# First pairs of a retention and feed-forward kernel: q loaded and transposed like k, zero products in fp32, first weight casts in halves

## The chip, the core and the metric

The kernel runs on one core of one Trainium2 chip. The metric is the device time of one execution in microseconds (us), as the median of several runs of the same program. The engines are TensorE (PE, its weight loads shown as PEld), VectorE (DVE), ScalarE (ACT), GpSimd (POOL) and SyncE (SP), which here only issues transfers. Matrix products write to PSUM, the accumulator memory; everything else lies in SBUF or in device memory.

## What is computed

A decayed linear attention (one decay per head), and then a bilinear feed-forward over its tokens:

```python
gamma = 1.0 - 2.0 ** (-5.0 - np.arange(H))          # q, k, v: [4, 8, 768, 64]
for t in range(S):
    state = gamma[None, :, None, None] * state + np.einsum('bhd,bhe->bhde', k[:, :, t], v[:, :, t])
    y[:, :, t] = scale * np.einsum('bhd,bhde->bhe', q[:, :, t], state)
x = y.transpose(0, 2, 1, 3).reshape(B * S, H * D)   # [3072, 512]
out = (x @ w_a) * (x @ w_b) @ w_out                 # w_a, w_b: [512, 1536]; w_out: [1536, 512]
```

All inputs and the output are fp32; the products on TensorE take bf16 operands.

## The kernel before

**Tiling.** The 3072 tokens are 24 slots of 128 tokens, six for each batch entry. The decay is put into the operands: k is multiplied by gamma to the power of -(t - 384) and q by gamma to the power of (t - 384) over 8, from tables (`ktab`, `qtab`), so that within a batch entry attention is a masked product of q and k (`scores`), its product with v (`intra`), and the product of q with a running state (`inter`, `update`). The feed-forward goes over token tiles of `TILES = [4, 2, 4, 4, 4, 4, 2]` slots: for each of 12 blocks of the inner dimension `ffn_a` and `ffn_g` make the two products (four TensorE instructions each, ACT copies the one, DVE multiplies it with the other), and `ffn_out` makes the output rows of a slot from the 12 blocks.

**The first batch entry** is treated in three pairs of slots (`load_pair`, `casts2`, `flip2`, `scores2`, `update2`, `inter2`, `intra2`, `leave2`), 256 tokens each. k and v are loaded with two neighbouring tokens to a partition (`(p two)`, pieces of 512 bytes), so that a half of a pair is the even or the odd tokens (`par`). q is loaded otherwise: partition (b, h) holds 16 consecutive tokens of one head (NJ = 16; two transfers of 256 KB each with pieces of 2 KB, lines 96 to 102). Its scaling (line 240) takes its factors from a table with one row to such a partition, which `lane_table` (lines 158 to 179) makes from the identity matrix, and it is transposed by plain products with a selecting matrix `pick` (line 394): 32 weight loads and 32 products to a pair, against 8 and 8 for k (line 387). The columns of q's transposed tile, and so those of the scores, of the attention's result and the rows of the output tile, stand in (j, b) order; `masks` and the output's address pattern follow that.

**Output rows.** The six slots of the first two token tiles are stored in that permuted order through SP's queue. `ffn_out` puts such a store in `held` (line 529), and `store` issues it at the next step. The others go through ACT's queue.

**What sets the order.** Each engine works strictly in the order in which the program is written: `seq` ties every instruction to the one before on its engine. SP's order matters too, since all loads, the permuted stores and the DMA transposes (line 261, slots from 10 on) stand in one queue: `LOADS` gives the first part, and `casts` issues the load of slot t + 2 behind the transpose of slot t. In the feed-forward of later token tiles, `todo` says before which step the attention of two slots (`turn`) runs; `turn(12, 10)` stands before step 9 of token tile 2 and needs the transposes of slots 12 and 13.

**The start.** The pairs 0 and 1 and the first weights are loaded first (k, q, v, k, q, v, then `w0` as two transfers of 512 KB for w_a and w_b). `warm` puts products of zeros (line 472, bf16, 512 columns) where TensorE would wait; their results are not used. `cast_w` (line 217) casts a chunk of 256 columns of w_a and w_b on POOL, one instruction of 128x1024 for each; the first `ffn_a` waits for the first of them. DVE scales k and q of pair 0, POOL k of pair 1, DVE q of pair 1.

Of the kernel before, what the change touches and what calls it, by code (L numbers as in the profile page):

```python
# [9 lines left out]
F32 = mybir.dt.float32  # L10
# [6 lines left out]
PAIRS = 3  # L17
# [7 lines left out]
def kernel(  # L25
# [26 lines left out]
    NJ = 16  # L52
# [41 lines left out]
    def load_pair(u):  # L94
        for nm, src in (("k", k), ("q", q), ("v", v)):
            if nm == "q":
                f = raws[nm, "pair", u] = raw.tile([P, NJ, D], F32, tag="qf", name="qf")
                s = q[0, :, 2 * u * P : 2 * (u + 1) * P, :].rearrange("h (b j) d -> b h (j d)", j=NJ)
                for x in range(2):
                    xs = slice(x * NJ // 2 * D, (x + 1) * NJ // 2 * D)  # L100
                    seq(nc.sync.dma_start(out=f.rearrange("p j d -> p (j d)")[:, xs], in_=s[:, :, xs]))  # L101
                continue
            f = raw.tile([P, H, 2, D], F32, tag=nm + "f", name=nm + "f")
            s = src[0, :, 2 * u * P : 2 * (u + 1) * P, :].rearrange("h (p two) d -> p h two d", two=2)
            seq(nc.sync.dma_start(out=f, in_=s))  # L105
            for par in range(2):
                raws[nm, 2 * u + par] = f[:, :, par, :]
# [23 lines left out]
    kqb = {}  # L131
    issue_loads(6)
    zero = const.tile([P, HP, P], BF16, name="zero")
# [10 lines left out]
    def tables(pattern, channel):  # L144
# [9 lines left out]
        if channel == 1:  # L154
            seq(nc.scalar.activation(qtab[:, :, :, 0], earg, AF.Exp, bias=bq))
        tabs.append((ktab, qtab))

    def lane_table():
        row = const.tile([P, PAIRS, NJ], F32, name="row")
        seq(nc.gpsimd.iota(row, pattern=[[2 * P, PAIRS], [1, NJ]], base=-MID, channel_multiplier=0,  # L160
                           allow_small_or_imprecise_dtypes=True))
        start = const.tile([P, NJ, 1], F32, name="start")
        seq(nc.gpsimd.iota(start, pattern=[[NJ, NJ], [0, 1]], base=0, channel_multiplier=0,
                           allow_small_or_imprecise_dtypes=True))
        make_identity(nc, ident)
        lane = ident.rearrange("p (b h) -> p b h", h=H)
        own = const.tile([P, 2, 1], F32, name="own")
        for i, val in enumerate((start, lgr)):
            one = const.tile([P, NJ, H], F32, name=f"one{i}")
            seq(nc.vector.tensor_tensor(one, lane, val.to_broadcast([P, NJ, H]), op=ALU.mult))  # L170
            seq(nc.vector.tensor_reduce(out=own[:, i], in_=one.rearrange("p b h -> p (b h)"),
                                        axis=mybir.AxisListType.X, op=ALU.add))
        seq(nc.vector.tensor_scalar(row, row, own[:, 0], own[:, 1], op0=ALU.add, op1=ALU.mult))
        tab = const.tile([P, PAIRS, NJ, 1], F32, name="lanes")
        seq(nc.scalar.activation(tab[:, :, :, 0], row, AF.Exp, bias=bq))
        for r in range(2):
            seq(nc.vector.tensor_copy(pick[:, r],
                                      lane[:, :, HP * r : HP * r + HP].rearrange("p b h -> p h b")))
        return tab

    tables([[2 * P, PAIRS], [1, 2], [0, 1]], 2)
    pick = const.tile([P, 2, HP, NJ], BF16, name="pick")
    lanes = lane_table()
# [52 lines left out]
    def scaled(eng, t, i):  # L236
        ktab, qtab = tabs[0] if t < 2 * PAIRS else tabs[1]
        if i == 1 and t < 2 * PAIRS:
            u, js = t // 2, slice(NJ // 2 * (t % 2), NJ // 2 * (t % 2) + NJ // 2)
            seq(eng.tensor_tensor(ql[u][:, js], raws["q", "pair", u][:, js],  # L240
                                  lanes[:, u, js].to_broadcast([P, NJ // 2, D]), op=ALU.mult))
            return
# [124 lines left out]
    kT2, qT2, ql = {}, {}, {}  # L367

    def casts2(u, on):
        for t in (2 * u, 2 * u + 1):  # L370
            new_nat(t)
        ql[u] = nat.tile([P, NJ, D], BF16, tag="ql", name="ql", bufs=2)
# [5 lines left out]
    def flip2(u, i, on):  # L378
        if i == 0:
            kT2[u] = tra.tile([P, 2, HP, P], BF16, tag="kT2", name="kT2", bufs=2)  # L380
            qT2[u] = tra.tile([P, NJ, HP, NJ], BF16, tag="qT2", name="qT2", bufs=2)
        for pars, eng in on:
            if i == 0:
                tp = psff.tile([P, 2, HP, P], BF16, tag="ff", name="tp")[:, : len(pars)]
                for m, par in enumerate(pars):
                    for hp in range(HP):
                        seq(nc.tensor.transpose(tp[:, m, hp, :], kb[2 * u + par][:, hp, :, :], ident))
                cast(eng, kT2[u][:, pars[0] : pars[0] + len(pars)], tp)
            else:
                tq = psff.tile([P, NJ // 2, HP, NJ], F32, tag="ff", name="tq")  # L390
                j0 = NJ // 2 * pars[0]
                for j in range(NJ // 2):
                    for r in range(2):
# [268 lines left out]
```

## Time and profile before

| what | value |
|---|---|
| time, three runs | 237.4, 237.82, 239.72 us |
| median | 237.82 us |
| span of the profiled execution | 236.9 us |
| mean granted TensorE clock over the span | 0.986 |
| TensorE instructions in the program: loads, products | 2160, 2160 |
| instructions issued by SP for pairs 0 to 2: k, q, v | 1, 2, 1 transfers a pair |
| feed-forward begins | 19.10 us into the span |

The span reaches from the first to the last instruction of one profiled execution; its own time is not listed apart, and the median of the runs is 0.9 us above the span. A page of the profile gives busy time for each engine, the chain of work that ended last, groups of instructions by line, and transfers. A row of the timeline reads: start, duration, engine, line, operation, output and input, number of instructions merged, and in brackets how long the engine had been idle and what released it. "issue" in the brackets means that it waited for nothing that the profile shows. In a table of stretches each engine has its busy time and number of instructions, and the last three columns are the granted TensorE clock (1.00 is full speed), the mean busy share of the 16 DMA engines and GB/s.

### The profile page before, as it was taken

To read this page: it belongs to the slowest core of one execution; us is meant where nothing else is said; L and a number is where in the kernel's file an instruction comes from. 1 tells how busy PE (TensorE), PEld (TensorE's weight loads), DVE (VectorE), ACT (ScalarE), POOL (GpSimd) and SP (SyncE) were. 2 spreads that over 40 slices of the span, in tenths; PEclk is the share of its full clock that TensorE was granted. 3 is DMA by queue.
4 is the path that set the end of the run, shared out by engine and by line. 5 is a ranking of instruction groups with operands and counts; after the bars stand their busy time and mean duration, and the time that the engine had idled before them with its cause. 6 is when DMAs were issued, how large, how long until landed. Compare 5 with 4: busy or idle time off the path is not lost.

```text
span 236.9 us, 5206 instructions
## 1 busy us (share of the span) xinstructions
PE 227.1 (96%) x2138; PEld 123.9 (52%) x2160; DVE 98.6 (42%) x177; ACT 84.6 (36%) x165; POOL 79.0 (33%) x100
## 2 busy tenths in 40 slices
PE   7869998999999999999999999999999999999994
PEld 2546644579555544545454544454544444445874
DVE  6774436655264046634045640155630134310430
ACT  3343334433123433514234431344512243312422
POOL 6247647786774224646444540000000000000000
PEclk9995999999999999999999999999999999999999
DMA  6999999999999999999999993200002200012102
GB/s 167 260 308 349 349 243 351 377 218 205 222 223 236 195 254 183 229 181 264 246 254 163 236 153 105 89 4 0 3 0 89 89 3 0 0 47 89 44 3 89
DMA packets 89640, 38.61 MB, mean 163 GB/s; under 512 B 71825, under 2 KB 84369, under 8 KB 89617
## 3 DMA queue, kind: packets, MB, share of 16 engines
q1 hardware_dynamic: 87024, 33.69, 69.3%
q10 hardware_dynamic: 2592, 4.59, 5.3%
q8 instruction: 17, 0.28, 0.5%
q14 instruction: 7, 0.05, 0.1%
HBM read 28.31 MB, written 6.29 MB: 146 GB/s over the span
## 4 chain that ended last, share of the span: by engine, by line
PE 88%; DMA 4%; SPq 3%; issue 1%; DVE 1%; ACT 1%; POOL 0%; ACTq 0%; DVEq 0%
PE o L521 26%; PE a L486 26%; PE g L496 26%; DMA wsta<-in_moe_w_a_dram 4%; PE at L290 2%; SPq L101 2%; PE y L335 2%; PE st L306 2%; SPq L105 1%; PE y L452 1%; PE y L326 1%; DVE ql L240 1%; PE y L440 1%; POOL wa_bf L215 0%; PE tp L272 0%
## 5 line engine op out<-in xcount | busy, mean ns | idle before, releaser
L498 DVE TENSOR_TENSOR ht<-g,asb 128x512 bf16<-128x512 f32 (+1 forms) x86 | 52.0, 604 | 108.6 <-PE g L496 89.9
L486 PE MATMUL a<-xt,wa_bf 128*128 128x512 bf16 (+1 forms) x337 | 76.7, 347 | 0.8 <-POOL wa_bf L215 0.3
L496 PE MATMUL g<-xt,wb_bf 128*128 128x512 bf16 (+1 forms) x341 | 76.2, 346 | 0.4 <-ACT asb L489 0.2
L489 ACT CAST asb<-a 128x512 bf16<-128x512 f32 (+1 forms) x86 | 44.4, 517 | 69.6 <-PE a L486 67.9
L521 PE MATMUL o<-wo_bf,ht 128*128 128x512 bf16 (+2 forms) x303 | 63.7, 362 | 0.5
L496 PEld LDWEIGHTS <-wb_bf 128*128 128x128 bf16 x344 | 33.8, 99 | 29.0 <-issue 0.4
L486 PEld LDWEIGHTS <-wa_bf 128*128 128x128 bf16 x344 | 33.0, 99 | 28.2 <-POOL wa_bf L215 0.5
L521 PEld LDWEIGHTS <-ht 128*128 128x128 bf16 x312 | 29.2, 98 | 31.4
L247 POOL TENSOR_TENSOR kqb<-kf,ktab 128x512 bf16<-128x512 f32 x22 | 22.9, 1043 | 33.3 <-DMA kf<-in_k_dram 30.4
L213 ACT COPY osb<-o 128x512 f32<-128x512 f32 (+2 forms) x25 | 14.1, 565 | 53.5 <-PE o L521 38.0
L295 DVE TENSOR_TENSOR aT<-at,mask 128x512 bf16<-128x512 f32 x36 | 22.3, 680 | 0.0
L215 POOL CAST vb<-vf 128x512 bf16<-128x512 f32 x24 | 15.0, 631 | 17.9 <-DMA vf<-in_v_dram 12.6
L247 POOL TENSOR_TENSOR kqb<-qf,qtab 128x512 bf16<-128x512 f32 x18 | 18.8, 1043 | 2.4 <-DMA qf<-in_q_dram 1.3
L344 ACT CAST xt<-y 128x512 bf16<-128x512 f32 x18 | 9.7, 589 | 3.0 <-PE y L335 3.0
L472 PE MATMUL idle<-zero 128*128 128x512 bf16 x21 | 8.2, 513 | 1.4 <-DVE zero L134 1.3
L414 DVE TENSOR_TENSOR aT<-at,mask 128x512 bf16<-128x512 f32 x12 | 7.5, 682 | 2.7 <-PE at L408 2.7
L215 POOL CAST wa_bf<-wsta 128x1024 bf16<-128x1024 f32 x6 | 6.7, 1117 | 3.6 <-DMA wsta<-in_moe_w_a_dram 3.6
L215 POOL CAST wb_bf<-wstb 128x1024 bf16<-128x1024 f32 x6 | 6.2, 1041 | 2.5 <-DMA wstb<-in_moe_w_b_dram 2.5
L215 POOL CAST wo_bf<-wsto 128x1024 bf16<-128x1024 f32 x6 | 6.3, 1042 | 1.9 <-DMA wsto<-in_moe_w_out_dram 1.9
L213 ACT CAST gst<-st 128x256 bf16<-128x256 f32 x12 | 4.5, 372 | 6.7 <-PE st L306 6.7
L432 ACT CAST gbd<-st 64x256 bf16<-64x256 f32 x10 | 3.7, 367 | 6.3 <-PE st L427 6.2
L290 PE MATMUL at<-kqT 64*64 64x128 bf16 x288 | 5.8, 219 | 0.0
(61 smaller groups left out, 92.8 us busy)
## 6 DMA issues: line engine op xcount, KB each, us to landing
qf<-in_q_dram SPq DMA_DIRECT2D x24, 256.0 KB, 5.2
kf<-in_k_dram SPq DMA_DIRECT2D x18, 256.0 KB, 4.7
vf<-in_v_dram SPq DMA_DIRECT2D x18, 256.0 KB, 5.1
out_dram<-osb ACTq DMA_DIRECT2D x17, 256.0 KB, 2.0
wsta<-in_moe_w_a_dram SPq DMA_DIRECT2D x6, 512.0 KB, 9.2
wstb<-in_moe_w_b_dram SPq DMA_DIRECT2D x6, 512.0 KB, 9.3
wsto<-in_moe_w_out_dram SPq DMA_DIRECT2D x6, 512.0 KB, 8.9
kf<-in_k_dram SPq DMA_DIRECT2D x3, 512.0 KB, 7.9
```

The lines of the kernel that those rows point to most:

```text
L213: seq(nc.scalar.copy(dst, src))
L215: seq(engine.tensor_copy(dst, src))
L247: seq(eng.tensor_tensor(dst, src, tab, op=ALU.mult))
L290: seq(nc.tensor.matmul(at[r][half(c), hp, :], kqT[t][half(r), 0, hp, half(c)], kqT[t][half(r), 1, hp, :], start=True, stop=True, skip_grou ...
L295: seq(nc.vector.tensor_tensor(aT[t][:, r], at[r], mask.to_broadcast([P, HP, P]), op=ALU.mult))
L344: seq(nc.scalar.copy(xt[J][:, 2 * r : 2 * r + 2, i * P : (i + 2) * P].rearrange("p j (s n) -> p j s n", s=2), ys[t // 2][r].rearrange("p ( ...
L472: seq(nc.tensor.matmul(idle, zero[:, 0, :], zero, start=True, stop=True, skip_group_check=True))
L486: seq(nc.tensor.matmul(a, wa_bf[:, kt, fs], xcols(J, kt, c0, c1), start=(kt == 0), stop=(kt == KT - 1)))
L489: seq(nc.scalar.copy(asb, a))
L496: seq(nc.tensor.matmul(g, wb_bf[:, kt, fs], xcols(J, kt, c0, c1), start=(kt == 0), stop=(kt == KT - 1)))
L498: seq(nc.vector.tensor_tensor(ht[J][:, ft, c0:c1], g, asbs.pop((J, ft, c0)), op=ALU.mult))
L521: seq(nc.tensor.matmul(o, ht[J][:, ft, i * P : (i + 1) * P], wo_bf[:, ft, c0:c1], start=(ft == 0), stop=(ft == NFT - 1)))
```

## The change

Line numbers in the text are those of the program before. Four things are done:

- q of the three pairs is loaded, scaled and transposed as k is: one transfer of 512 KB with pieces of 512 bytes, scaling from `qtab`, four transposes to a half pair. `lane_table` and `pick` are gone. Columns now stand in (par, m) order, token 2m + par, and masks, scores, `inter2` and the output's address pattern follow it.
- The zero products are fp32, 256 columns, and 13 instead of 24.
- The transposes of k of pair 0 and their copies are split in two halves, odd tokens first.
- The casts of the first weight chunk are done in halves of 128 columns.

```diff
     def load_pair(u):
         for nm, src in (("k", k), ("q", q), ("v", v)):
-            if nm == "q":
-                f = raws[nm, "pair", u] = raw.tile([P, NJ, D], F32, tag="qf", name="qf")
-                s = q[0, :, 2 * u * P : 2 * (u + 1) * P, :].rearrange("h (b j) d -> b h (j d)", j=NJ)
-                for x in range(2):
-                    xs = slice(x * NJ // 2 * D, (x + 1) * NJ // 2 * D)
-                    seq(nc.sync.dma_start(out=f.rearrange("p j d -> p (j d)")[:, xs], in_=s[:, :, xs]))
-                continue
...
-    zero = const.tile([P, HP, P], BF16, name="zero")
+    zero = const.tile([P, 2 * P], F32, name="zero")
...
-        if channel == 1:
-            seq(nc.scalar.activation(qtab[:, :, :, 0], earg, AF.Exp, bias=bq))
+        seq(nc.scalar.activation(qtab[:, :, :, 0], earg, AF.Exp, bias=bq))
...
-    pick = const.tile([P, 2, HP, NJ], BF16, name="pick")
-    lanes = lane_table()
+    make_identity(nc, ident)
...
-                                        base=-par, pattern=[[0, 1], [1, NJ], [NJ, 8]],
+                                        base=-par, pattern=[[0, 1], [1, 2], [2, 64]],
...
-    def cast_w(j):
-        sl = slice(j * WC, (j + 1) * WC)
-        cast(nc.gpsimd, wa_bf[:, :, sl], wst["a", j])
-        cast(nc.gpsimd, wb_bf[:, :, sl], wst["b", j])
+    def cast_w(j, parts=1):
+        for nm, dst in (("a", wa_bf), ("b", wb_bf)):
+            for x in range(parts):
+                a, b = x * WC // parts, (x + 1) * WC // parts
+                cast(nc.gpsimd, dst[:, :, j * WC + a : j * WC + b], wst[nm, j][:, :, a:b])
...
     def flip2(u, i, on):
-        if i == 0:
-            kT2[u] = tra.tile([P, 2, HP, P], BF16, tag="kT2", name="kT2", bufs=2)
-            qT2[u] = tra.tile([P, NJ, HP, NJ], BF16, tag="qT2", name="qT2", bufs=2)
+        into = (kT2, qT2)[i]
+        if u not in into:
+            into[u] = tra.tile([P, 2, HP, P], BF16, tag="kq"[i] + "T2", name="kq"[i] + "T2", bufs=2)
         for pars, eng in on:
...
-                for j in range(NJ // 2):
-                    for r in range(2):
-                        seq(nc.tensor.matmul(tq[half(r), j], ql[u][:, j0 + j, :], pick[:, r],
-                                             start=True, stop=True, skip_group_check=True))
-                cast(eng, qT2[u][:, j0 : j0 + NJ // 2], tq)
+            tp = psff.tile([P, 2, HP, P], BF16, tag="ff", name="tp")[:, : len(pars)]
+            for m, par in enumerate(pars):
+                for hp in range(HP):
+                    seq(nc.tensor.transpose(tp[:, m, hp, :], kqb[2 * u + par][:, i, hp, :, :], ident))
+            cast(eng, into[u][:, pars[0] : pars[0] + len(pars)], tp)
...
-                                         qT2[u][half(r), :, hp, 8 * c : 8 * c + 8],
+                                         qT2[u][half(r), :, hp, half(c)],
...
     def warm(n, pool, tag):
-        idle = pool.tile([P, HP, P], F32, tag=tag, name="idle")
+        idle = pool.tile([P, 4 * P], F32, tag=tag, name="idle")
         for _ in range(n):
-            seq(nc.tensor.matmul(idle, zero[:, 0, :], zero, start=True, stop=True,
+            seq(nc.tensor.matmul(idle[:, : 2 * P], zero[:, :P], zero, start=True, stop=True,
                                  skip_group_check=True))
...
-                held.append((dst.rearrange("(b j) d -> j b d", j=NJ), src))
+                held.append((dst.rearrange("(m par) d -> par m d", par=2), src))
...
-    warm(11, psat, "y1")
+    warm(6, psat, "y1")
     casts2(0, {(K, 1): D_, (K, 0): D_, (Q, 0): D_, (Q, 1): D_})
-    flip2(0, K, [((0, 1), A_)])
-    warm(3, psat, "y1")
-    flip2(0, Q, [((0,), D_)])
+    flip2(0, K, [((1,), A_), ((0,), A_)])
+    warm(2, psat, "y1")
+    flip2(0, Q, [((0,), A_)])
     warm(1, psat, "y1")
-    flip2(0, Q, [((1,), A_)])
-    warm(3, psat, "y1")
+    flip2(0, Q, [((1,), D_)])
+    warm(1, psat, "y1")
     scores2(0, 1)
     scores2(0, 0, True)
     update2(0, 0)
-    warm(4, psat, "y1")
+    warm(2, psat, "y1")
...
-    warm(2, psff, "ff")
+    warm(1, psff, "ff")
...
-    cast_w(0)
+    cast_w(0, 2)
```

More of the change, by code (lines that the diff above doesn't have):

```diff
@@ L51 @@
     MID = S // 2
-    NJ = 16
     lg = [math.log(1.0 - 2.0 ** (-5.0 - h)) for h in range(H)]
@@ L130 @@
     kqb = {}
-    kqb = {}
     issue_loads(6)
-    zero = const.tile([P, HP, P], BF16, name="zero")
+    zero = const.tile([P, 2 * P], F32, name="zero")
     seq(nc.vector.memset(zero, 0.0))
@@ L153, in tables @@
         seq(nc.scalar.activation(ktab[:, :, :, 0], earg, AF.Exp, scale=-1.0))
-        if channel == 1:
-            seq(nc.scalar.activation(qtab[:, :, :, 0], earg, AF.Exp, bias=bq))
+        seq(nc.scalar.activation(qtab[:, :, :, 0], earg, AF.Exp, bias=bq))
         tabs.append((ktab, qtab))
[L158 to L175, printed above, removed]
-        for r in range(2):
-            seq(nc.vector.tensor_copy(pick[:, r],
-                                      lane[:, :, HP * r : HP * r + HP].rearrange("p b h -> p h b")))
-        return tab
     tables([[2 * P, PAIRS], [1, 2], [0, 1]], 2)
-    pick = const.tile([P, 2, HP, NJ], BF16, name="pick")
-    lanes = lane_table()
+    make_identity(nc, ident)
     gbd = [const.tile([P, HP, P], BF16, name=f"gbd{i}") for i in range(2)]
@@ L237, in scaled @@
         ktab, qtab = tabs[0] if t < 2 * PAIRS else tabs[1]
[L238 to L242, printed above, removed]
         dst, src, tab = kqb[t][:, i], raws["kq"[i], t], (ktab, qtab)[i][:, t % NCH]
@@ L364, in turn @@
             leave(old)
-    kT2, qT2, ql = {}, {}, {}
+    kT2, qT2 = {}, {}
     def casts2(u, on):
@@ L371, in casts2 @@
             new_nat(t)
-        ql[u] = nat.tile([P, NJ, D], BF16, tag="ql", name="ql", bufs=2)
         for (i, par), eng in on.items():
@@ L441, in inter2 @@
                                          gbd[c][:, hp, half(r)],
-                                         qT2[u][:, :, hp, 8 * c : 8 * c + 8], start=False, stop=False,
+                                         qT2[u][:, :, hp, half(c)], start=False, stop=False,
                                          skip_group_check=True))
```

10 lines of the change are left out of this document (removed).

## The prediction

> **What bounds the kernel now.** I read the page first, then the timeline of the first 27 us, the stretches around the place where the clock changes, and last the stretch where the permuted stores go out.
>
> ```profile
> span 236.9 us, 5206 instructions
> ...
> PE 227.1 (96%) x2138; PEld 123.9 (52%) x2160; DVE 98.6 (42%) x177; ACT 84.6 (36%) x165; POOL 79.0 (33%) x100
> ...
> PE 88%; DMA 4%; SPq 3%; issue 1%; DVE 1%; ACT 1%; POOL 0%; ACTq 0%; DVEq 0%
> ```
>
> TensorE carries 88% of the chain that ended last. The other 12% is the start: loads, then the first weight chunk. So a saving in the start is worth what it brings forward the stretch that TensorE then fills without a gap.
>
> ```profile
> 5.32 1.29 DVE L247 TENSOR_TENSOR kqb<-kf,ktab 128x512 bf16<-128x512 f32 x2 [0.35 <-ACT ktab L153]
> ...
> 7.64 0.69 DVE L240 TENSOR_TENSOR ql<-qf,lanes 128x512 bf16<-128x512 f32 x1 [0.42 <-DMA qf<-in_q_dram]
> ...
> 9.24 1.17 POOL L215 CAST vb<-vf 128x512 bf16<-128x512 f32 x2 [4.51 <-DMA vf<-in_v_dram]
> ...
> 11.40 2.04 POOL L247 TENSOR_TENSOR kqb<-kf,ktab 128x512 bf16<-128x512 f32 x2 [0.99 <-DMA kf<-in_k_dram]
> ...
> 15.24 1.17 POOL L215 CAST vb<-vf 128x512 bf16<-128x512 f32 x2 [1.80 <-DMA vf<-in_v_dram]
> ...
> 17.70 0.74 PE L408 MATMUL at<-qT,kT 64*64 64x128 bf16 x17 [1.41 <-issue]
> 18.00 1.04 POOL L215 CAST wa_bf<-wsta 128x1024 bf16<-128x1024 f32 x1 [1.59 <-DMA wsta<-in_moe_w_a_dram]
> ...
> 19.10 1.03 PE L486 MATMUL a<-xt,wa_bf 128*128 128x256 bf16 x4 [0.33 <-POOL wa_bf L215]
> 19.51 1.04 POOL L215 CAST wb_bf<-wstb 128x1024 bf16<-128x1024 f32 x1 [0.46 <-DMA wstb<-in_moe_w_b_dram]
> ...
> 26.60 1.04 PE L486 MATMUL a<-xt,wa_bf 128*128 128x512 bf16 x4
> ```
>
> The releases in brackets date the landings: k of pair 0 by 5.3 us, q by 7.6, v by 9.2, k of pair 1 by 11.4, q and v of pair 1 by 15.2, the first weights by 18.0. POOL then casts 1.04 us and the feed-forward begins at 19.10. At 17.70 the second pair's scores resume after 1.41 us in which TensorE waited for nothing that the profile shows ("issue").
>
> ```profile
> core 0: us, PE busy (x) PEld busy (x) DVE busy (x) ACT busy (x) POOL busy (x), PEclk, DMA share, GB/s
> 0.00:10.27 10.27, 8.42 (x89) 3.70 (x92) 6.49 (x27) 3.93 (x7) 4.70 (x20) 1.00 0.87 210
> ...
> 0.00:17.69 17.69, 13.56 (x220) 7.06 (x223) 12.73 (x35) 7.38 (x14) 8.04 (x24) 0.99 0.97 245
> 13.79:17.20 3.41, 1.73 (x50) 1.13 (x49) 2.72 (x5) 1.99 (x3) 1.17 (x2) 1.00 1.11 339
> ...
> 17.20:20.60 3.40, 2.57 (x53) 1.77 (x53) 1.89 (x3) 1.10 (x3) 2.08 (x2) 0.50 1.10 348
> ...
> 18.00:24.00 6.00, 5.67 (x94) 4.00 (x83) 2.58 (x4) 2.06 (x5) 4.17 (x4) 0.50 1.10 349
> 24.00:26.00 2.00, 2.00 (x20) 1.79 (x19) 1.27 (x3) 0.47 (x2) 1.41 (x2) 1.00 1.10 348
> ```
>
> TensorE was busy only 1.73 of the 3.41 us before 17.2, and after that its granted clock is 0.50 until 24.0. The feed-forward runs its first 4.9 us (19.1 to 24.0) at half speed. The wait at 17.70 comes after 220 + 223 = 443 TensorE instructions.
>
> ```profile
> q8 instruction: 17, 0.28, 0.5%
> ```
>
> Seventeen instruction packets of 16 KB for 2138 + 2160 = 4298 instructions are about 253 a packet. I read the wait as TensorE waiting for such a packet: the limits then lie near instructions 190, 443 and 700. Instruction 190 passed at about 10.35 us (181 by 10.27), so a packet took about 7.35 us from the limit that asks for it to the restart.
>
> The Trainium skill, "Runtime: NRT & Kernel Launch", Instruction fetch mechanics, also gives 16 KiB blocks of 256 instructions, but calls a crossing mostly hidden; by that, fewer instructions are worth nothing. The trace differs: 1.41 us at this place.
>
> **The change part by part.** *Fewer TensorE instructions.* In the listing of the two programs each pair's q goes from 32 loads and 32 products to 8 and 8 (48 fewer, 96 in two pairs), and the zero products from 24 pairs to 13 single instructions (35 fewer): 131. What was instruction 443, in the scores of pair 1, is now 312, and the limit falls in `inter2(1)`, behind the first feed-forward product. The limit near 190 moves from 10.35 to about 11.9 us (`intra2(0, 1)`); plus 7.35 that is 19.25, and by the start worked out below TensorE would be there at about 18.95. So a wait of 0.3 us remains (bounds 0 and 1.4). The products themselves are cheap both ways:
>
> ```profile
> 6.67 0.73 PE L387 MATMUL tp<-ident,kqb 128*128 128x128 bf16 x8 [0.54 <-DVE kqb L247]
> ...
> 1.25 4.88 PE L472 MATMUL idle<-zero 128*128 128x512 bf16 x11 [1.25 <-DVE zero L134]
> ```
> ```profile
> L215 POOL CAST vb<-vf 128x512 bf16<-128x512 f32 x4 | 2.3, 614 | 6.3 <-DMA vf<-in_v_dram 6.3
> ...
> L213 ACT COPY kT<-tp 128x1024 bf16<-128x1024 bf16 x2 | 2.0, 1012 | 3.0 <-PE tp L387 3.0
> ...
> L215 DVE CAST qT<-tq 128x512 bf16<-128x512 f32 x3 | 2.0, 689 | 0.1
> ...
> L213 ACT CAST xt<-y 128x512 bf16<-128x512 f32 x3 | 1.7, 593 | 1.8 <-PE y L452 1.8
> ```
>
> Eight transposes take 0.73 us, as k shows. An fp32 zero product has no row. From below, half of a bf16 one's 0.44 us (4.88 over 11; half the columns); from above, four times that for the wider type, 0.9 us. I take 0.8, because thirteen of them then fill about the time of twenty-four. They stand where TensorE waits for DVE or ACT; six end at about 6.1 us, before both halves of k are scaled (5.32 + 1.29 = 6.61). At 0.9 they cost 0.1 us there, which the first weights at 18 us hide.
>
> *q like k.* From the landings: k to q of pair 0 took 7.6 - 5.3 = 2.3 us, q to v 1.6, v to k 2.2, k to v (with q between) 3.8, so q of pair 1 about 2.2 if v took 1.6 again. All are 512 KB. As a load of k's form q should take 1.6 to 2.2; I take 1.8, nearer to the mean of its neighbours, and 0.45 less per pair, 0.9 before the first weights (bounds 0 and 1.3). Two issues on SP's queue go too. DVE scales q with the same shape as k, 0.69 us each. ACT copies kT of pair 0 in two halves (0.59 each by ACT's xt row, against 1.01 for one): 0.17 us more of ACT, but the first half starts sooner. q's copies on DVE are kept at 0.69. The lane table's DVE and POOL work lay before k's landing at 5.3 and saves nothing.
>
> *Half casts.* POOL takes 0.61 us for 128x512 against 1.04 for 128x1024, so the first product may start 0.43 us sooner; the two halves of a tile take 1.22, still under the 1.5 us between two landings (18.00 to 19.51), so nothing queues behind them on POOL. The start of the feed-forward: 19.10 - 0.9 - 0.43 = 17.77.
>
> *Clock.* Without the 1.41 us hole TensorE is about 1.4 us busier in the stretch that ends the full clock: 3.1 of 3.41, less 0.4 for q's shorter products. I take it that the clock then holds. The 4.9 us at half clock shrink by 2.45.
>
> *Pair 2.* The loads come about 1.3 us earlier, TensorE 3.5 us earlier:
>
> ```profile
> 34.74 2.04 POOL L247 TENSOR_TENSOR kqb<-kf,ktab 128x512 bf16<-128x512 f32 x2 [1.85 <-DMA kf<-in_k_dram]
> ...
> 41.04 0.69 PE L394 MATMUL tq<-pick,ql 128*64 128x64 bf16 x32 [0.87 <-DVE ht L498]
> ```
>
> k of pair 2 is scaled by about 36.8 - 1 = 35.8, while TensorE arrives near 35.2: a wait of 0.6 us, in part in place of the 0.87 before q. I take 0.3 us given back (bounds 0 and 1.2). q's 32 products (0.69) become 8 transposes, 0.25 less.
>
> *The sum*: -1.33 (start) - 2.45 (clock) + 0.3 (the moved instruction packet) + 0.3 (pair 2) - 0.25 = -3.4 us. The span goes from 236.9 to 233.5. The median of the runs shown, 237.82, is 0.9 above the span, so 234.4.
>
> **Rivals.** *The clock falls all the same* (at 0.50 until 24.0). Then the 1.33 us won at the start buy 0.67 us of full-speed work, less the same 0.35 net: about 237.4. For it speaks that the half clock came with a stretch 51% busy and stayed through 17.2 to 20.6, 76% busy, so the threshold is unknown. The Trainium skill, "TensorE: Matmul & The Clock Gate", Part 4, says that transposes don't count as busy for the clock; this change puts transposes in place of plain products. No run here shows that yet. The same 237 us comes out if each fp32 product were issued as several instructions, so that the early count hardly falls.
>
> *The new stores pile up on few DMA engines.* With columns in (par, m) order a store of the first six token tiles changes from 16 runs of 8 rows to 2 runs of 64 rows (out_dram 16x8x512 to 2x64x512). If a transfer is dealt out over the engines by its first dimension, two engines carry each store.
>
> ```profile
> q10 hardware_dynamic: 2592, 4.59, 5.3%
> ...
> out_dram<-osb ACTq DMA_DIRECT2D x17, 256.0 KB, 2.0
> ```
> ```profile
> 66.74 1.06 SPq L509 DMA_DIRECT2D out_dram<-osb  x1
> ...
> 87.59 2.41 SPq L261 DMA_TRANSPOSE kqT<-kqb  x1
> ```
> ```profile
> DMA to landing us min/median/max: 4.6/5.1/5.9
> ```
> ```profile
> 97.45 0.64 PE L290 MATMUL at<-kqT 64*64 64x128 bf16 x32
> ```
> ```profile
> 66.00:72.00 6.00, 5.95 (x73) 3.37 (x63) 3.94 (x7) 1.12 (x3) 4.30 (x5) 1.00 1.33 205
> ...
> 90.00:96.00 6.00, 6.00 (x29) 2.74 (x28) 3.14 (x6) 1.89 (x4) 3.06 (x5) 1.00 1.37 183
> ```
>
> The stores on ACT's queue (q10) show the price of a 2 KB packet: 5.3% of 16 x 236.9 us over 2592 packets is 77.5 ns. A store of 128 packets is 0.62 us over 16 engines and 4.96 over two: 4.3 more, 26 us for six. The transposes and slot loads stand behind them in SP's queue, and the engines have nothing to spare there (share above 1). The transpose issued at 87.59 lands by 93.5 at the latest and is wanted at 97.45. 26 us later, less 1.5 for the earlier start, it lands at 118: TensorE stands 20.5 us, restarts at half clock for some 3.4 us (1.7 lost), and the time is 236.9 + 20.5 + 1.7 + 0.9 = 260 (253 to 266). It decides from the point where more than 4 us are added ahead of that transpose. Against it: nothing in this trace shows a transfer on fewer engines, since every one here has a first dimension of 16 or 128; the nearest row (the same store at 16) says no cost, which is why I keep it as a rival. For it: a store's 128 packets need 9.9 us of engine time yet land in 2.0 us elsewhere, so some rule does deal them out.
>
> The Trainium skill, "DMA: Bandwidth & Descriptors", Why a DMA increments its semaphore by 16 and not by 1, states that rule: the largest number up to 16 that divides the slowest dimension of both sides, here 2. By it the time is the 260 above.
>
> *The zero products don't hold the clock early*, and both pairs run at half clock: the first feed-forward product starts perhaps 1.5 us later than before, 239.5.
>
> **How the numbers follow.** Forecast 0.41, clock falls 0.16, stores on two engines 0.37, early clock lost 0.06. The runs shown spread by 1%, so 1% (2.4 us) is what can be told from no change. Faster by more than that means below 235.4: most of the forecast's 0.41 (its own range is 233 to 236.5) and a little of the second, 0.40. Within 1%: 0.16. Slower: 0.44. The cases lie on both sides, so the range runs from 233 into the store case, to 263; it leaves out its upper tail and the times below 233.
>
> **What would show it.** Right: the "issue" wait at the scores of pair 1 is gone, the first feed-forward product starts near 17.8 us, the clock stays 1.00 from 18 to 24 us, and the wide products begin near 23 us rather than 26.6. Wrong in the store: landings of the permuted stores well over 5 us, later landings of the transposes behind them, and a hole in TensorE in the second or third token tile, waiting for kqT. Wrong in the clock: 0.50 again in the first 24 us.

## The result, and the profile after

The changed kernel takes 259.6 us (median of four runs, 258.98 to 261.92) against 237.6 us (236.96 to 239.72) for the kernel before, run beside it. The ratio is 1.0907, with a 95% interval from 1.0825 to 1.0988: the change makes the kernel about 9%, or 22 us, slower. The forecast of 234.4 us was wrong. The rival of the stores that pile up on two DMA engines, 260 us, came out.

Lines of the changed kernel are numbered anew: L438 and L448 are the feed-forward's products (L486 and L496 before), L252 the scores of a slot (L290), L461 the permuted store (L509), L223 the DMA transpose (L261), L179 ScalarE's copies (L213), L181 the casts (L215), L360 the scores of a pair (L408), L424 the zero products (L472).

From the page of the changed kernel: the span, then TensorE's busy tenths, its granted clock and the DMA engines' share, each in 40 slices of 6.4 us, and the chain that ended last by engine.

```profile
span 257.5 us, 5083 instructions
...
PE   7969999999993996029996999999999999999995
...
PEclk9997999999999799558999999999999999999999
DMA  6999999999979459399999999320000310003102
...
PE 70%; SPq 12%; DMA 12%; ACT 1%; issue 1%; DVE 1%; POOL 1%; ACTq 0%; POOLq 0%; DVEq 0%
```

TensorE has two holes, one near 80 us (the 3) and one from 97 to 116 us (6, 0, 2). The DMA engines are far from full behind the first and in the second: the digits 4, 5 and 3 stand for 84 to 97 and 103 to 109 us, where the kernel before shows 9 without a break up to 140 us. TensorE's share of the chain falls from 88 to 70%; DMA and SyncE's queue now carry 24% of it, 7% before.

The waits of TensorE say on whom (engine and line, waited for: us in total, times, longest).

```profile
PE at L252 <- DMA kqT<-kqb: 13.1, 1, 13.1
PE a L438 <- ACT osb L179: 4.5, 1, 4.5
PE g L448 <- ACT asb L441: 2.7, 2, 2.4
PE a L438 <- POOL wa_bf L181: 1.9, 1, 1.9
```

The first two are new and the third was 0.2 us: 13.1 us for a transpose, 4.5 us behind ScalarE's copy of an output tile, and 2.4 us once more behind ScalarE. The timeline shows how the first two come from the stores (start, duration, engine, line; in brackets the idle time before and who ended it). The 2.4 us fall near 139 us, long after these stores, and are of the kind that the filled hole shows below: ScalarE's store at 138.69 waited for a load that landed at 138.61.

```profile
64.43 0.88 SPq L461 DMA_DIRECT2D out_dram<-osb  x1
65.42 4.11 SPq L223 DMA_TRANSPOSE kqT<-kqb  x1
...
75.28 1.18 SPq L461 DMA_DIRECT2D out_dram<-osb  x2
76.58 8.56 SPq L223 DMA_TRANSPOSE kqT<-kqb  x1
...
83.54 0.59 ACT L179 COPY osb<-o 128x512 f32<-128x512 f32 x1 [7.27 <-DMA out_dram<-osb]
84.18 1.86 PE L438 MATMUL a<-xt,wa_bf 128*128 128x512 bf16 x4 [4.49 <-ACT osb L179]
...
89.95 4.91 SPq L461 DMA_DIRECT2D out_dram<-osb  x3
...
95.04 9.89 SPq L223 DMA_TRANSPOSE kqT<-kqb  x1
...
109.37 2.19 SPq L223 DMA_TRANSPOSE kqT<-kqb  x1
...
113.99 1.07 PE L252 MATMUL at<-kqT 64*64 64x128 bf16 x32 [13.13 <-DMA kqT<-kqb]
```

The first two-run store is issued at 64.43. By its semaphore (the counter that a transfer raises when it lands) it lands at 73.1, after 8.7 us, and the other five take 8.2 to 16.5 us, where the stores before landed in 4.4 (the page's median). There are four output buffers. The copy at 83.54 is the sixth into them, and it had to wait for the second store, which was issued at 75.28 and landed at 83.4. ScalarE stands meanwhile, and TensorE behind it. The transposes that follow the stores in SyncE's queue take 4.1, 8.6 and 9.9 us to issue alone (1.5 to 2.6 for the same ones before). The fourth, which the scores want, is issued at 109.37 and lands at 113.95, 20.5 us later than before (93.46), and the scores start at 113.99, after a wait of 13.1 us. In four stretches of the windows (span, busy time and count of each engine, granted clock, DMA share, GB/s):

```profile
84.00:90.00 6.00, 5.82 (x21) 2.32 (x21) 2.03 (x3) 1.79 (x4) 0.00 (x0) 0.74 0.45 100
...
102.00:108.00 6.00, 0.00 (x0) 0.00 (x0) 0.00 (x0) 0.00 (x0) 0.00 (x0) 0.68 0.45 51
108.00:114.00 6.00, 0.01 (x4) 0.01 (x4) 0.00 (x0) 0.00 (x0) 2.70 (x3) 0.50 1.27 228
114.00:120.00 6.00, 6.00 (x85) 3.69 (x86) 3.17 (x5) 2.03 (x4) 2.70 (x3) 0.68 1.36 182
```

After each hole the clock has fallen as well: it is 0.74 in the stretch after the first and 0.68 in the one after the second.

The start, for which the change was otherwise costed, shows the gain of the first product that was expected, and about half of what was expected by the wide products:

```profile
1.25 4.81 PE L424 MATMUL idle<-zero 128*128 128x256 f32 x12 [1.25 <-DVE zero L125]
...
14.86 0.64 PE L360 MATMUL at<-qT,kT 64*64 64x128 bf16 x32
...
16.93 1.18 POOL L181 CAST wa_bf<-wsta 128x512 bf16<-128x512 f32 x2 [1.61 <-DMA wsta<-in_moe_w_a_dram]
17.60 0.61 PE L438 MATMUL a<-xt,wa_bf 128*128 128x256 bf16 x4 [1.86 <-POOL wa_bf L181]
...
24.50 1.04 PE L438 MATMUL a<-xt,wa_bf 128*128 128x512 bf16 x4
```

The scores of pair 1 run through without the wait of 1.41 us, the first feed-forward product starts at 17.60 instead of 19.10, and the wide ones at 24.50 instead of 26.60 (predicted near 23).

### The profile page after: what moved, and what is told of

The parts are those of the page before. It is cut to its first block, busy times and chain, and to the rows that moved or that the text cites. A ratio compares the mean times of both kernels' runs of the same rounds, so it can differ in the third digit from the quotient of the medians.

```text
span 257.5 us, 5083 instructions
## 1 busy us (share of the span) xinstructions
PE 230.3 (89%) x2090; PEld 126.9 (49%) x2090; DVE 95.5 (37%) x170; ACT 84.4 (33%) x166; POOL 78.5 (30%) x100
## 4 chain that ended last, share of the span: by engine, by line
PE 70%; SPq 12%; DMA 12%; ACT 1%; issue 1%; DVE 1%; POOL 1%; ACTq 0%; POOLq 0%; DVEq 0%
PE a L438 22%; PE g L448 21%; PE o L473 19%; SPq L223 6%; DMA wsta<-in_moe_w_a_dram 3%; DMA out_dram<-osb 3%; SPq L97 3%; SPq L91 3%; DMA qf<-in_q_dram 2%; PE at L252 2%; DMA kqT<-kqb 2%; PE y L297 2%; DMA kf<-in_k_dram 2%; PE st L268 1%; PE y L288 1%
## 5 line engine op out<-in xcount | busy, mean ns | idle before, releaser
L438 PE MATMUL a<-xt,wa_bf 128*128 128x512 bf16 (+1 forms) x344 | 78.3, 351 | 6.4 <-ACT osb L179 4.5
L448 PE MATMUL g<-xt,wb_bf 128*128 128x512 bf16 (+1 forms) x344 | 77.5, 350 | 2.7 <-ACT asb L441 2.7
L438 PEld LDWEIGHTS <-wa_bf 128*128 128x128 bf16 x344 | 33.1, 99 | 35.3 <-issue 6.5
L448 PEld LDWEIGHTS <-wb_bf 128*128 128x128 bf16 x344 | 34.1, 100 | 32.5 <-issue 4.5
L179 ACT COPY osb<-o 128x512 f32<-128x512 f32 (+2 forms) x25 | 14.1, 565 | 57.6 <-PE o L473 38.3
L257 DVE TENSOR_TENSOR aT<-at,mask 128x512 bf16<-128x512 f32 x36 | 22.3, 681 | 13.3 <-PE at L252 13.3
L181 POOL CAST vb<-vf 128x512 bf16<-128x512 f32 x24 | 15.0, 631 | 13.7 <-DMA vf<-in_v_dram 9.4
L252 PE MATMUL at<-kqT 64*64 64x128 bf16 x288 | 6.2, 229 | 13.1 <-DMA kqT<-kqb 13.1
L179 ACT CAST gst<-st 128x256 bf16<-128x256 f32 x12 | 4.5, 372 | 22.1 <-PE st L268 20.1
L252 PEld LDWEIGHTS <-kqT 64*64 64x64 bf16 x288 | 4.7, 113 | 13.6 <-DMA kqT<-kqb 13.2
L424 PE MATMUL idle<-zero 128*128 128x256 f32 x26 | 9.1, 488 | 1.3 <-DVE zero L125 1.3
L181 POOL CAST wa_bf<-wsta 128x1024 bf16<-128x1024 f32 (+1 forms) x7 | 6.8, 982 | 3.3 <-DMA wsta<-in_moe_w_a_dram 3.3
L181 POOL CAST wb_bf<-wstb 128x1024 bf16<-128x1024 f32 (+1 forms) x7 | 6.4, 921 | 2.2 <-DMA wstb<-in_moe_w_b_dram 2.2
L424 PEld LDWEIGHTS idle<-zero 128*128 128x128 f32 x26 | 5.8, 244 | 2.3 <-DVE zero L125 1.2
```

Of the source, the lines that this page charges most:

```text
L179: seq(nc.scalar.copy(dst, src))
L181: seq(engine.tensor_copy(dst, src))
L252: seq(nc.tensor.matmul(at[r][half(c), hp, :], kqT[t][half(r), 0, hp, half(c)], kqT[t][half(r), 1, hp, :], start=True, stop=True, skip_grou ...
L257: seq(nc.vector.tensor_tensor(aT[t][:, r], at[r], mask.to_broadcast([P, HP, P]), op=ALU.mult))
L424: seq(nc.tensor.matmul(idle[:, : 2 * P], zero[:, :P], zero, start=True, stop=True, skip_group_check=True))
L438: seq(nc.tensor.matmul(a, wa_bf[:, kt, fs], xcols(J, kt, c0, c1), start=(kt == 0), stop=(kt == KT - 1)))
```

## The experiments

Theory one: a store whose first dimension is 2 runs on two DMA engines, and this alone makes the 22 us and more; the rest of the change is worth 2 to 3 us. Rivals: rows written 4 KB apart are slow as such; the loss comes from other edits; it comes from the order of SyncE's queue or from the output buffers, not from the load of two engines. Ratios are to the kernel before, run beside each group, with 95% intervals. In the three groups that kernel took 239.2, 239.5 and 238.7 us, so runs of different groups are compared by their ratios and not by their times.

**Split stores.**

```diff
-                held.append((dst.rearrange("(m par) d -> par m d", par=2), src))
+                rows = dst.rearrange("(m par) d -> par m d", par=2)
+                for par in range(2):
+                    held.append((rows[par], src[half(par)]))
```

> Each permuted store of the first six token tiles goes out as two transfers of 64 rows each (one for each parity), so that the first dimension is 64 and not 2; rows, bytes and queue stay as in the changed kernel. Theory one (a transfer's first dimension of 2 puts it on two DMA engines, and that is the whole loss): the landings fall from 25 to 44 us to some 5 us, the hole at 102 to 114 us goes, and what is left is the gain of the start (wide feed-forward products at 24.5 instead of 26.6 us, less the transposes of pair 2): 234 to 236 us. Rival (rows written 4 KB apart are slow as such, or the loss comes from another edit): 256 to 260 us. If more transfers on the queue cost something: 236 to 239 us.

235.55 us, ratio 0.9867 (0.9814 to 0.992). The same rows go to the same places from the same queue, only twelve transfers instead of six (one for each slot of the first two token tiles); 24 us are gone, and the kernel is about 1% faster than before. By their semaphores the twelve land in 2.3 to 4.6 us. (The landings of 25 to 44 us in the expectation were misread: those of the changed kernel are the 8.2 to 16.5 us above.) TensorE's list of waits is now:

```profile
PE a L438 <- POOL wa_bf L181: 1.8, 1, 1.8
PE idle L424 <- DVE zero L125: 1.3, 1, 1.3
PE g L448 <- ACT asb L441: 0.2, 1, 0.2
```

Row distance and row order are ruled out as the cause, and so are the other edits, all of which are still in it.

**The kernel before with two-run stores.**

```diff
-                held.append((dst.rearrange("(b j) d -> j b d", j=NJ), src))
+                held.append((dst.rearrange("(b j) d -> j b d", j=2), src))
```

> The kernel before with one edit: its permuted stores are written as 2 runs of 64 rows instead of 16 runs of 8, so rows land in another order; nothing else is changed. Theory one: six stores get some 4.3 us longer each, the same hole in TensorE as in the changed kernel appears, 257 to 262 us. Rival (the loss comes from the loads, casts or transposes of the first pairs): 237 to 239 us.

260.31 us, ratio 1.0941 (1.0882 to 1.1). This one line, put alone into the kernel before, costs the whole loss; its TensorE too waits 13.2 us for kqT.

**More runs to a store.** The changed kernel with `par=4`, and with `par=8`.

> The changed kernel with the permuted stores written as 4 runs of 32 rows (rows land in another order). Theory one, by which the first dimension is the number of engines: a store takes 2.5 us of each of four engines instead of 5 us of each of two, 1.9 us more than over sixteen, 11 us for six; the late transpose is then some 7 us late and the time 240 to 246 us. Rival (any permuted row order is slow, or few long runs are not the cause): 255 to 260 us. If the two-engine cost were a fixed one that falls away above two: 234 to 236 us.

> The changed kernel with the permuted stores written as 8 runs of 16 rows (rows land in another order). If the first dimension is the number of engines: a store takes 1.24 us of each of eight, 0.6 us more than over sixteen, 3.7 us for six, which the slack of the transposes hides for the most part: 235 to 239 us. If something else than the number of engines made four runs cost 13 us (long runs, the row order): 241 to 246 us.

248.59 us, ratio 1.0448 (1.0374 to 1.0522), and 241.92 us, ratio 1.0153 (1.0096 to 1.0209). Both are above the range of theory one, so its sizes were too low, and eight runs fell into the rival's range. With the kernel of plain stores below (ratio 0.9899) as the case of sixteen engines, and 237.8 us for a ratio of 1, the excess is:

| runs to a store | excess over plain stores | six stores' time on an engine, less that at sixteen |
|---|---|---|
| 2 | 24.0 us | 26.0 us |
| 4 | 13.1 us | 11.2 us |
| 8 | 6.0 us | 3.7 us |

The third column is the prediction's price (128 packets of 77.5 ns over k engines, six times) with nothing taken off for slack. The excess falls by about half at each doubling, less steeply than the third column, and stays within 2.3 us of it; the slack by which I lowered the expectations for 4 and 8 was not there. TensorE's waits for kqT and for an output buffer together are 17.6, 8.6 and 1.6 us with 2, 4 and 8 runs. So part of the 6.0 is not shown to be the stores': with eight runs TensorE also stands 4.3 us behind ScalarE in a way that other kernels show too (below).

```profile
PE g L448 <- ACT asb L441: 4.5, 2, 4.3
PE a L438 <- POOL wa_bf L181: 1.9, 1, 1.9
PE at L252 <- DMA kqT<-kqb: 1.6, 1, 1.6
```

That the runs set the number of engines can be read in the traces too, from how often a store's semaphore is signalled. The first store of the changed kernel has three signals: one at 65.7 us, soon after its issue, and two at 73.1, at its landing. With four runs each store has five signals, with eight nine (one of 54 is missing from that trace), and in the kernel before and with plain stores sixteen. One signal early and one at the landing for each run is what 2, 4 and 8 engines would give.

**Queue or engines.** Two-run stores issued on ScalarE's queue, first with four output buffers, then with seven, and seven buffers with the stores in SyncE's queue.

```diff
         for dst, src in held:
-            seq(nc.sync.dma_start(out=dst, in_=src))
+            seq(nc.scalar.dma_start(out=dst, in_=src))
...
-    osbp = ctx.enter_context(tc.tile_pool(name="osbp", bufs=4))
+    osbp = ctx.enter_context(tc.tile_pool(name="osbp", bufs=7))
```

> The changed kernel with the same two-run stores, issued by ScalarE on its queue instead of SyncE's, at the same places of the program. If the loss goes through the order of SyncE's queue (transposes and loads behind the stores), the transposes no longer wait and the time is 235 to 241 us. If the load of the two engines decides, whichever queue the stores are in, since the transposes are dealt over the same engines: 250 to 260 us.

> Two-run stores on ScalarE's queue, as in the run before, with 7 output buffers instead of 4, so that none of the six waits for a store. If the load of two engines delays whatever is dealt over all sixteen (loads and transposes alike): 248 to 258 us, with TensorE waiting for loads or kqT in place of osb. If the time on ScalarE's queue was lost to the buffers alone: 235 to 240 us.

> The changed kernel with 7 output buffers instead of 4. The 6.9 us that TensorE waits behind osb go. If the transposes behind the stores decide (26 us of two engines' time stand ahead of the transpose in either case): the wait for kqT grows by about as much and the time stays at 256 to 260 us. If the two waits add: 252 to 254 us.

260.41 us (ratio 1.0911, 1.0812 to 1.101), 258.7 us (1.082, 1.0751 to 1.0889) and 259.75 us (1.0884, 1.0816 to 1.0951), the first two just above the range of the loaded engines. Neither another queue nor more buffers, nor both, wins more than about 2 us. With seven buffers and the stores in SyncE's queue, the wait behind `osb` (4.5 of the 6.9 us that the expectation put there) is gone and that for kqT has grown by 5 us:

```profile
PE at L252 <- DMA kqT<-kqb: 18.1, 2, 12.1
PE g L448 <- ACT asb L441: 2.2, 2, 2.0
```

So these two waits are two outlets of one delay. With the stores on ScalarE's queue and seven buffers, no store stands ahead of a transpose in SyncE's queue, and the transposes are late nevertheless:

```profile
70.35 6.47 SPq L223 DMA_TRANSPOSE kqT<-kqb  x1
...
93.66 0.58 ACT L179 COPY osb<-o 128x512 f32<-128x512 f32 x1 [13.82 <-DMA kqT<-kqb]
94.30 1.87 PE L438 MATMUL a<-xt,wa_bf 128*128 128x512 bf16 x4 [12.95 <-ACT osb L179]
```

By the trace's semaphores the transpose issued at 70.35 lands at 86.6, after 16 us (the four of the kernel before whose rows start between 67 and 88 us take 4.6 to 5.9). The loads of k and q issued at 76.86 and 77.49 take 13.3 and 13.5 us (medians before: 4.7 and 5.2). What transposes and loads share with these stores is the engines. The stores stand alone in ScalarE's queue here, which shows how few engines carry them: the 128 packets of the first took 13.4 us together and ran within 7.4 us, on 1.8 engines in the mean, where 128 packets of a plain store at 163 us took 11.0 us together and ran within 0.8. ScalarE then waits for a transpose before its next store goes out, for the reason shown below.

**Order restored at the copy, plain stores.** The rows are put in order where y is copied into `xt`, and a store is one plain transfer of 128 rows.

```diff
-            cast(eng, xt[J][:, i + c], ys[u][c])
+            cast(eng, xt[J][:, i + c].rearrange("p kt (m par) -> p kt par m", par=2),
+                 ys[u][c].rearrange("p kt (par m) -> p kt par m", par=2))
...
-                held.append((dst.rearrange("(m par) d -> par m d", par=2), src))
+                held.append((dst, src))
```

> The changed kernel, but the rows are put in order where ScalarE copies the first pairs' y into xt (the columns of each tile written with a stride of 2), and the stores are then plain ones of 128 rows. If the two-engine stores are the whole loss: as with split stores, 234 to 237 us, where a strided copy that takes longer than 0.6 us, six times in the chain of the first pairs, may add up to 1 us.

236.87 us, ratio 0.9899 (0.9851 to 0.9947): as expected.

**The hole before the first weights filled.** On top of the split stores.

```diff
     cast_w(0, 2)
     W2 = 2 * P
+    warm(2, psff, "ff")
```

> The kernel with split stores, and two more fp32 zero products (four passes, some 1.4 us) in the 1.8 us in which TensorE waits for the first weights. If that hole is what lets the clock fall in 18 to 24 us: the granted clock stays 1.00 there, the wide products begin near 23.0 instead of 24.5 us and the time is 1 to 1.5 us under that with split stores (234.0 to 234.6). Rival (the dip comes with the transposes and narrow products of the stretch before, or by chance of where the clock's windows fall): the mean clock in 18 to 24 us stays near 0.75 and the time does not move.

237.69 us, ratio 0.994 (0.9906 to 0.9973). The first half of the expectation came: the clock is 1.00 from 18 to 24 us, and the wide products start at 23.04. But by the ratios the time is 1.7 us above that of the split stores alone, with intervals that just overlap. The timeline near 115 us and a stretch of the windows show where the gain went:

```profile
112.07 0.58 ACT L179 COPY osb<-o 128x512 f32<-128x512 f32 x1 [2.00 <-PE o L473]
...
116.38 0.34 ACTq L485 DMA_DIRECT2D out_dram<-osb  x1
...
116.76 1.07 ACT L441 CAST asb<-a 128x512 bf16<-128x512 f32 x2 [4.10 <-DMA kf<-in_k_dram]
...
117.39 1.86 PE L448 MATMUL g<-xt,wb_bf 128*128 128x512 bf16 x4 [2.77 <-ACT asb L441]
```
```profile
116.00:122.00 6.00, 4.61 (x15) 1.84 (x15) 1.63 (x3) 1.66 (x3) 2.90 (x4) 0.72 1.19 240
```

ScalarE has its copy done at 112.65 and issues the store only at 116.38; everything behind it waits, TensorE 2.8 us. The clock falls with that wait too (0.72 from 116 to 122 us, 1.00 there with the split stores alone), which costs up to some 1.7 us more. The store has nothing to do with k. But the trace names the semaphore of each transfer. In this program the transfers of all queues share eight of them, and a store waits for the landing of the transfer that had its semaphore before:

```
kernel             store on ScalarE's queue   same semaphore before it             landed
before             117.13                     qf load issued at 111.51             117.06
filled hole        107.35                     vf load issued at 101.80             107.28
filled hole        116.38                     kf load issued at 112.24             116.30
split stores       114.15                     a store issued at 107.24             112.10
```

In the kernel before, the copy ended at 117.01 and the load landed at 117.06, so it did not show. A TensorE that comes earlier runs into it; with the split stores the semaphores fell otherwise.

**Third tile's stores on SyncE's queue as well.** On top of the filled hole.

```diff
             if J < 2:
...
+            elif J == 2:
+                held.append((dst, src))
             else:
                 seq((nc.sync if c0 else nc.scalar).dma_start(out=dst, in_=src))
```

> The kernel with split stores and the filled hole, and the four plain stores of the third token tile issued by SyncE in the program's later places, as those of the first two tiles are, instead of by ScalarE. In the run with the filled hole such a store held ScalarE for 4.1 us (112.7 to 116.4 us) until a load that had used the same semaphore had landed, and TensorE stood 2.8 us behind it. If that wait is what ate the gain of the start: it goes, and the time is 2 to 4 us under the run with the filled hole (233.5 to 235.5). Rival (the loads and transposes themselves set the pace near 115 us): SyncE's queue waits instead and the time stays at 236.5 to 238.5 us.

234.1 us (233.48 to 234.29), ratio 0.9819 (0.979 to 0.9849), ahead of both kernels and of the filled hole alone; it is the lowest ratio of all, but its interval overlaps with that of the split stores. ScalarE's wait is gone, and TensorE stands nowhere for more than 1.2 us; from the page, its busy tenths, and from its waits the longest:

```profile
PE   7999999999999999999999999999999999999994
```
```profile
PE idle L424 <- DVE zero L125: 1.2, 1, 1.2
PE tp L347 <- DVE ht L450: 0.5, 1, 0.5
```

Its profiled execution also began earlier than that of the filled hole (first feed-forward product at 16.82 instead of 17.70 us, with the same start of the program), so the gain is read from the six times, not from the span.

**Single parts of the start.** Split stores with the first weights cast whole (`cast_w(0)`), and the kernel before with the halves alone.

> The kernel with split stores, with the first weights cast whole instead of in halves. If the halves bring the first feed-forward product forward by 0.43 us (1.04 against 0.61 us of cast): it starts 1.04 us or a little more after the landing of the first weights instead of 0.6, near 18.2 us, and the time is 0.4 us longer, too little to be told from the ratio. Rival (the second matrix's cast or the landing sets the pace): the wide products start no later than with halves, at 23.0 us with full clock or 24.5 us with the dip.

> The kernel before with the first weights cast in halves and nothing else: q stays in lanes, with its 16-run loads, its 32 products for each pair and bf16 zero products. If the change's early gain is the sum of 0.9 us from q's loads and 0.43 us from the halves: the first feed-forward product starts near 18.7 us, between 19.1 before and 17.6 to 17.9 with the change, and the wait at the scores of the second pair (0.9 to 1.4 us, released by nothing that the profile shows) stays. Rival (the loads are no faster in the new form): it starts near 17.9 us. Time 236.5 to 238.5 us.

236.15 us, ratio 0.9925 (0.9887 to 0.9963), and 239.29 us, ratio 1.0038 (0.9996 to 1.008). With whole casts the first feed-forward product starts at 18.22, as expected, and the wide ones at 25.17, in a profile with the dip; by the ratio this kernel cannot be told from the split stores with halves. The lane kernel with halves, from its timeline and its waits:

```profile
17.17 0.46 PE L409 MATMUL at<-qT,kT 64*64 64x128 bf16 x17 [1.17 <-issue]
...
18.33 0.61 PE L487 MATMUL a<-xt,wa_bf 128*128 128x256 bf16 x4 [0.49 <-ACT gbd L433]
...
23.80 1.04 PE L487 MATMUL a<-xt,wa_bf 128*128 128x512 bf16 x4
```
```profile
PE g L497 <- ACT asb L490: 4.3, 2, 4.1
```

The "issue" wait stays with q in lanes, as expected. The wide products are 2.8 us earlier than before, and yet the time is not lower: TensorE waits 4.1 us behind ScalarE near 119 us, again for a store that is held (issued at 118.76, when a load with the same semaphore had landed at 118.68). That would explain a time above the range expected; no run of this kernel without the held store shows it.

## Why the prediction was wrong, point by point

**The step that failed** is the store. The sum had no term for the edit of `held.append`: it was left at the price of the row before, because "the nearest row (the same store at 16) says no cost, which is why I keep it as a rival". That row has a first dimension of 16, so it could not tell a price at 2. The step of the rival was right in its mechanism: a transfer's first dimension sets how many engines carry it. One line put into the kernel before costs 9%, and taking it out of the changed kernel gives them back. By the Trainium skill, "DMA: Bandwidth & Descriptors", Why a DMA increments its semaphore by 16 and not by 1, the engines are the largest number up to 16 that divides the slowest dimension of both sides; the runs with 2, 4, 8 and 64 or 128 rows agree, with 24.0, 13.1, 6.0 us over plain stores. With that row counted for nothing, the chances (0.41 for the forecast, 0.37 for this rival) should have stood the other way round.

**The rival's size.** Predicted were 26 us on two engines ahead of one transpose, less 1.5 us for the start, so that TensorE stands 20.5 us and loses 1.7 us by the clock: 260. Measured, that transpose lands 20.5 us late and not 24.5. TensorE stands 13.1 us for it and 4.5 us through the four output buffers, which the prediction did not name; the run with seven buffers shows that these did not change the sum. Another 2.4 us come from a held store near 139 us. The clock of 0.74 and 0.68 after the holes takes some 3.5 us, twice the price. With 2.1 us won at the start that makes 21.4, and the span grew by 20.6. So the total of 260 is right with several terms off that cancel, which is luck; the cause that it names is right.

**Start.** The first product was put at 17.77 and starts at 17.60. Both terms came out. By the semaphores the first weights land at 17.6 to 18.2 us in the three profiles with q in lanes, and at 16.7 to 17.2 in nine with the new loads (at 15.4 in two more): 0.9 us or a little more, as predicted. From that landing the first product comes after 1.15 us with whole casts (17.95 to 19.10 before) and after 0.72 with halves (16.88 to 17.60): 0.43 less, as predicted.

**Instruction packet.** The wait at the scores of pair 1 went, as said, and the 0.3 us put at the moved limit do not show. But the count was off: the profile lists 26 zero products for 13, as one of the rivals allowed, so that 92 instructions fell away in the first two pairs and not 131. The wait went all the same. That TensorE waited for a packet stays a reading. The traces fit it: in the three profiles with the wait an instruction packet ends at 15.74 to 16.27 us, and TensorE resumes 1.4 to 1.6 us later.

**Clock.** It was said to hold if the 1.41 us hole is gone. In the changed kernel, with split stores and with the stores on ScalarE's queue and four buffers it dipped (0.72, 0.76 and 0.72 from 18 to 24 us), in four other profiles of the same start it held (four and eight runs to a store, and the two with seven buffers). The profile with four runs to a store, for one:

```profile
17.62 0.61 PE L438 MATMUL a<-xt,wa_bf 128*128 128x256 bf16 x4 [2.04 <-POOL wa_bf L181]
...
22.96 1.04 PE L438 MATMUL a<-xt,wa_bf 128*128 128x512 bf16 x4
```

From the same first product the wide ones start 1.5 us earlier than the changed kernel's 24.50, and at the predicted 23. And the lane kernel with halves held the clock with a hole of 1.17 us in it. So the hole does not decide; the prediction's reason falls, what decides stays open, and the term of 2.45 us is 2.1 where the clock holds (26.60 to 22.96, less 1.5 for the start) and 0.6 where it dips (26.60 to 24.50, less 1.5). The Trainium skill, "TensorE: Matmul & The Clock Gate", Part 1, What's actually happening, says that the window which judges activity runs freely and doesn't start with the kernel; the two outcomes of one start agree with it. The two profiles with the hole filled held the clock, which four without did too, so filling is not shown to help.

**The rest.** Without the store the sum was close: 234.4 predicted, 235.55 measured with split stores, and the ratio of 0.9867 makes 234.4 of the 237.6 us before. That is partly luck. In the profile with split stores the span is 3.0 us shorter (3.4 predicted), and two terms are off in opposite ways. The wide products are 2.1 us earlier, where the terms for start and clock add up to 3.8 us. The other 0.9 us come later: TensorE has no wait at pair 2, so that its 0.87 us before q are gone and the 0.3 us that were to be given back do not show.

## What to carry to other kernels

When a change rewrites the address pattern of a transfer, cost it as an edit of its own: read its first dimension, and let a row of another first dimension count for nothing. A transfer that must go out in few long runs is better issued as several, each with many rows in front; here two stores of 64 rows cost nothing where one of 2x64 cost 24 us. And follow a gain at the start to the next place where an engine that issues transfers can be held: here stores on ScalarE's queue waited for other transfers' landings, and where the wide products started 1.5 and 2.8 us earlier the time did not fall.

## What the runs showed of the hardware that was not expected

- An fp32 product of 128x256 is issued as two loads and two products: 26 of each for 13, six of them in 4.81 us, 0.80 us each, as taken. The Trainium skill, "FP8 and Floating Point Precision", TensorE Precision Notes, speaks of four passes for full fp32; the profile lists two.
- The first dimension of a store sets how many engines carry it: 2, 4 and 8 runs show 3, 5 and 9 signals at its semaphore, and with two runs 128 packets of 13.4 us together take 7.4 us.
- Stores on two engines delay transfers from another queue as well: 16 us for a transpose from issue to landing, with no store ahead of it in its own queue (4.6 to 5.9 before).
- In this program the transfers of all queues share eight semaphores, and an engine that issues a store stands until the transfer that last used its semaphore has landed: 3.7 us for ScalarE at 112.65 us in the kernel with the filled hole.
- The same first 17.6 us are followed by a clock of 0.72 or of 1.00 from 18 to 24 us, which is worth 1.5 us.
